# A retention and two mixture-of-experts layers on one core: the front recast in half columns, with its elementwise work off GpSimd

## The chip, the cores and the metric

The kernel runs on one core of a Trainium2 chip. The metric is the device time of one execution in microseconds (us); every time is of the whole kernel unless a stage is named. The engines are named as in the profile: PE (matrix), DVE (vector), ACT (scalar), POOL (GpSimd), SP (which here only issues DMAs). PE's weight loads have a row of their own, PEld.

## What is computed

Three layers follow each other. The first is a retention over two batches of eight heads, 768 steps, head size 64:

```python
for t in range(S):
    state = gamma[None, :, None, None] * state + np.einsum('bhd,bhe->bhde', k[:, :, t], v[:, :, t])
    y[:, :, t] = scale * np.einsum('bhd,bhde->bhe', q[:, :, t], state)
```

Its output, 1536 tokens of 512 numbers, goes to a layer of eight experts (512 to 1024 to 512, relu between). Each token goes to the expert with the largest gate logit (`x @ w_gate`), if that expert's capacity of 384 isn't used up by earlier tokens, and is scaled by the softmax of its logits. The third layer sums four experts of the same size over all tokens, weighted by given probabilities.

## The kernel before

Only the front differs, the part up to the first expert's first matmul. It works through twelve chunks of 128 tokens (six per batch), one iteration of a Python loop each; a f32 matmul appears as two records in PE's rows. The kernel's order is written out by hand: each engine executes its instructions in the order of the code, and waits by semaphore.

For a chunk i the stages are these, by the names of the functions:

- `st_v` multiplies v by a decay per token and head (vg), on POOL.
- `st_S` makes the scores of the eight heads: q and k of two heads lie in the two halves of the 128 partitions, so eight matmuls of 64 rows and 128 columns write two PSUM banks, the two heads of a pair side by side. DVE multiplies by the causal mask (sd).
- `st_U` adds k'v to a running state in PSUM, which ACT copies to `st`; the sixth chunk of a batch has none.
- `st_I` and `st_O` make the output O (transposed): first from the state and q (not in a batch's first chunk), then from sd and vg.
- `st_x` multiplies O by the gate table `gqs` of the chunk, of which there are six, one per chunk of a batch (xT): ACT copies O from PSUM, POOL multiplies; for the last two chunks DVE does both at once.
- `x_pe` multiplies xT by `iw`, identity and gate weights side by side, which gives the tokens in rows and the logits. `x_reduce` adds the four partial logits (two reductions and a step that adds them and takes the maximum), ACT copies the tokens to xk in two pieces, and a DMA writes them to DRAM (xd).
- `x_dve` finds the expert of each token (`ohs`), the running counts (`cum`) and token numbers by expert (`ohk`).
- `r_pe` and `r_dve` give each token its rank within its expert by two small matmuls (R) and compare it with slot numbers (`slot_at`); `g_pe` collects the token number of each slot (slot_ps).

Iteration `it` runs I, U, O and x of chunk it-1, then v of chunk it+1, S of chunk it, the loads of chunk it+3, x_pe of chunk it-2, g_pe of chunk it-4 and r_pe of chunk it-3. SP issues the loads in the code's order: qk (q and k transposed, 512 KB a chunk), kv (k and v in rows, 512 KB), the gate tables (256 KB each), then expert weights; qk and kv have five buffers each. PSUM's eight banks are four that rotate and four with fixed use (slot, u and the two of X). In iteration 8 the first expert weight is split into a high and a low part, ACT then DVE on 128x1024.

After the loop come the last chunks: `late` places tokens of the last two chunks directly, `fetched` those that an indirect DMA gathers from xd, and ACT and DVE split the result for the first expert. Behind that the experts' matmuls begin (`pair`), which the change leaves alone. Lines of the profile: S is L267, U L291, I L310, O L322, X L365, slot_ps L447, R L350 and L351, vg L251, the gate product L337 and L341, xk L384, the step that adds logits L389, the weight split L142 and L143.

## Time and profile before

| | |
|---|---|
| median of three runs | 734.7 us (733.98 to 735.59) |
| the profiled execution | 732.1 us, its span 730.3 us |
| PE busy | 718.0 us, 98% of the span |
| DVE, ACT, POOL busy | 470.6, 337.7, 203.1 us |
| bytes moved by DMA | 92.83 MB |

The span is the time from the first to the last instruction in the trace; what lies around it, 1.8 us in that execution, is start and end. A matmul's row shows when it starts and how long until its result is there; matmuls overlap, so the cost of a stage is read from its start to the start of the next, not from its duration. A number in brackets behind a row is the time for which the engine had nothing to execute before, and what ended that.

### The profile page before, as it was taken

What the parts mean: (1) busy time and instruction counts of PE and PEld (TensorE: products, weight loads), DVE (VectorE), ACT (ScalarE), POOL (GpSimd) and SP (SyncE); (2) the same over time, 40 slices, a digit from 0 to 9 for tenths busy, and PEclk for the clock granted to TensorE, in tenths of its full rate; (3) what the DMA queues carried; (4) which work ended last, traced back from release to release, by engine and by line L of the source; (5) the groups of instructions that cost most, each with busy time, mean ns of one, the idle gap of its engine ahead of it and who ended that gap; (6) DMA issues with size and microseconds to landing.
All of it is one profiled execution on the core that took longest, in us unless ns stands there. A gap on an engine that the chain in (4) does not pass through costs nothing.

```text
span 730.3 us, 11338 instructions
## 1 busy us (share of the span) xinstructions
PE 718.0 (98%) x4425; PEld 656.6 (90%) x4426; DVE 470.6 (64%) x777; ACT 337.7 (46%) x545; POOL 203.1 (28%) x193
## 2 busy tenths in 40 slices
PE   7998999999999999999999999999999999999997
PEld 5887999999999889998889998899998899988896
DVE  3888899898889736455733755763475464557334
ACT  2344677776656433344333445534444333443331
POOL 3653844442054102112332112223322121111103
PEclk9999999999999999999999999999999999999999
DMA  8984887686641310211221112122222312112002
GB/s 329 414 345 135 301 306 237 239 289 226 226 146 34 116 56 32 87 58 58 88 86 58 58 57 88 59 87 87 87 73 76 99 42 87 59 58 84 33 1 86
DMA packets 28026, 92.83 MB, mean 127 GB/s; under 512 B 4097, under 2 KB 4369, under 8 KB 27970
## 3 DMA queue, kind: packets, MB, share of 16 engines
q1 hardware_dynamic: 23042, 81.79, 32.4%
q0 software_dynamic: 3056, 7.05, 2.8%
q10 hardware_dynamic: 1872, 3.24, 1.2%
q8 instruction: 35, 0.57, 0.3%
q14 instruction: 21, 0.17, 0.1%
HBM read 85.72 MB, written 6.34 MB: 126 GB/s over the span
## 4 chain that ended last, share of the span: by engine, by line
PE 88%; DVE 1%; POOL 1%; ACT 0%; issue 0%; POOLq 0%; ACTq 0%
PE o L1213 35%; PE a L1057 17%; PE m L951 15%; PE b L1057 9%; PE m L954 7%; PE bb L1057 5%; POOL out_dram L1225 1%; PE ab L1057 0%; DVE x L856 0%; DVE X L869 0%; ACT X L865 0%; DVE c L1150 0%; POOLq L1410 0%; PE T L769 0%; ACT c L1088 0%
## 5 line engine op out<-in xcount | busy, mean ns | idle before, releaser
L1213 PE MATMUL o<-w,g_c 128*128 128x512 f32 x1152 | 267.4, 390 | 0.0
L1213 PEld LDWEIGHTS o<-w,g_c 128*128 128x128 f32 x1152 | 215.8, 188 | 43.8
L143 DVE TENSOR_TENSOR w<-raw,w 128x1024 fp32r<-128x1024 f32 x128 | 158.2, 1244 | 14.2 <-ACT w L142 14.1
L1057 PE MATMUL a<-X,w 128*128 128x384 f32 x720 | 145.0, 336 | 0.0
L158 POOL TENSOR_TENSOR t<-raw 128x512 f32<-128x512 f32 x28 | 38.8, 1386 | 346.4 <-DMA raw<-b 299.1
L1092 DVE TENSOR_TENSOR c<-b,c 128x384 f32<-128x384 f32 x30 | 16.7, 558 | 181.3 <-PE b L1057 181.3
L142 ACT CAST w<-raw 128x1024 fp32r<-128x1024 f32 x128 | 132.1, 1048 | 2.7 <-DMA raw<-a 1.5
L1057 PEld LDWEIGHTS a<-X,w 128*128 128x128 f32 x720 | 127.4, 188 | 2.6 <-DVE c L1092 0.3
L1088 ACT COPY c<-a 128x384 f32<-128x384 f32 x60 | 28.8, 479 | 196.4 <-PE a L1057 196.4
L1073 ACT ACTIVATE g_c<-c 128x384 fp32r<-128x384 f32 x96 | 50.4, 526 | 65.9 <-DVE c L1092 64.6
L951 PE MATMUL m<-xet,w 128*128 128x432 f32 x256 | 79.1, 371 | 0.8 <-PEq L636 0.8
L951 PE MATMUL m<-h,w 128*128 128x432 f32 x256 | 79.2, 371 | 0.0
L1057 PE MATMUL b<-X,w 128*128 128x384 f32 x360 | 72.0, 334 | 0.0
L954 PE MATMUL m<-h,w 128*128 128x216 f32 x256 | 66.8, 261 | 0.0
L954 PE MATMUL m<-xet,w 128*128 128x216 f32 x256 | 66.7, 261 | 0.0
L625 POOL DMA_INDIRECT xe<-xd,gidx x42 | 52.7, 1255 | 46.2 <-DVE xT L753 34.7
L1057 PEld LDWEIGHTS b<-X,w 128*128 128x128 f32 x360 | 63.5, 188 | 0.0
L1077 DVE SCALAR_TENSOR_TENSOR g_c<-c,g_c 128x384 fp32r<-128x384 f32 x96 | 52.9, 551 | 3.9
L951 PEld LDWEIGHTS m<-xet,w 128*128 128x128 f32 x256 | 48.0, 188 | 2.9 <-PEq L636 1.0
L951 PEld LDWEIGHTS m<-h,w 128*128 128x128 f32 x256 | 48.1, 188 | 1.9
L954 PEld LDWEIGHTS m<-h,w 128*128 128x128 f32 x256 | 48.9, 191 | 0.0
L954 PEld LDWEIGHTS m<-xet,w 128*128 128x128 f32 x256 | 48.9, 191 | 0.0
(158 smaller groups left out, 763.1 us busy)
## 6 DMA issues: line engine op xcount, KB each, us to landing
raw<-a SPq DMA_DIRECT2D x64, 512.0 KB, 4.8
raw<-b SPq DMA_DIRECT2D x64, 512.0 KB, 3.5
qk<-qkv SPq DMA_DIRECT2D x12, 512.0 KB, 8.3
kv<-qkv SPq DMA_DIRECT2D x12, 512.0 KB, 8.3
xd<-xk ACTq DMA_DIRECT2D x12, 256.0 KB, 6.0
gqs<-gqt SPq DMA_DIRECT2D x6, 256.0 KB, 7.5
xe<-xd,gidx POOLq DMA_INDIRECT x44, 4.8
iw<-cst SPq DMA_DIRECT2D x1, 272.0 KB
```

The costliest lines, as they stand in the source:

```text
L142: nc.scalar.copy(w[:, 0], r)
L143: nc.vector.tensor_tensor(out=w[:, 1], in0=r, in1=w[:, 0].bitcast(F32), op=ALU.subtract)
L158: eng.tensor_tensor(out=c[:, 0:2], in0=b[:, 2:4], in1=b[:, 1:3], op=sub)
L625: nc.gpsimd.indirect_dma_start(out=t[:, b], out_offset=None, in_=xq, in_offset=bass.IndirectOffsetOnAxis(ap=gidx[:, b, e:e + 1], axis=0),)
L951: nc.tensor.matmul(out=b2, lhsT=w[0], rhs=x, start=first, stop=last, skip_group_check=True)
L954: nc.tensor.matmul(out=b2[:, 0], lhsT=w[1], rhs=x[:, 0], start=False, stop=last, skip_group_check=True)
L1057: nc.tensor.matmul(out=bk[:, 0:HT], lhsT=w[:, sw, k], rhs=x[:, sx, k], start=(first and m == 0), stop=(m == len(steps) - 1), skip_group_ch ...
L1073: nc.scalar.activation(out=h2[:, 0], in_=src, func=AF.Relu)
L1077: nc.vector.scalar_tensor_tensor(out=h2[:, 1], in0=src, scalar=0.0, in1=h2[:, 0].bitcast(F32), op0=ALU.max, op1=ALU.subtract,)
L1088: nc.scalar.copy(t, bk[:, 0:HT])
L1092: nc.vector.tensor_tensor(out=t, in0=bk[:, 0:HT], in1=t, op=ALU.add)
L1213: nc.tensor.matmul(out=bk, lhsT=h2[:, sh, cols], rhs=w[:, sw, k], start=(q == 0 and m == 0 and (n, t) not in begun), stop=(m == 2), skip_g ...
```

## The change

- **Half columns.** S, X, R and slot_ps are made of matmuls that use 64 columns of the array each. S has sixteen (64 rows by 64 columns, the four quarters of the array in turn) instead of eight, X eight (128 rows by 64 columns) instead of four, R and slot_ps four each instead of two. U, I and O had 64 columns already.
- **Order.** S of chunk `it` stands first in its iteration, ahead of I, U and O of chunk it-1. R is written into X's bank, just ahead of X. kv is loaded two chunks ahead, qk three.
- **Off POOL.** vg of chunks 2 to 11 is eight ACT instructions of 64 columns (POOL for chunks 0 and 1); the gate product is DVE's for every chunk, straight from PSUM; ohk is ACT's.
- **Tables.** One gate table is loaded; POOL makes the other five from it by a factor per partition and head. `iw` is built on chip by two ACT copies out of a smaller table.
- **Smaller steps.** The logits are one reduction over four parts and one maximum, xk one copy; the slot comparison reads 16-bit numbers (`rnk16`). The first weight is split in four parts, one in each of iterations 7 to 10.
- **PSUM.** The front has pairs of banks for S, O and X, one of each, beside slot and u. Before the last chunk's X that pool is closed and another opened, whose tiles wait for the old tiles one by one.

The diff, without the constants' layout on the host:

```diff
-    banks = [f"bank{n}" for n in range(4)]
-    held = ["slot", "u", "x0", "x1"]
+    ph0 = sctx.enter_context(tc.tile_pool(name="ph0", bufs=1, space=PSUM))
+    ps = [fctx.enter_context(tc.tile_pool(name="psa", bufs=1, space=PSUM))]
...
+    def split_part(q):
+        if q == 0:
+            parts.append((raws.pop(0), pw.tile([P, 2, 1024], F32R, tag="w", name="w0")))
+        r, w = parts[0]
+        cols = slice(256 * q, 256 * q + 256)
+        nc.scalar.copy(w[:, 0, cols], r[:, cols])
+        nc.vector.tensor_tensor(
+            out=w[:, 1, cols], in0=r[:, cols], in1=w[:, 0, cols].bitcast(F32), op=ALU.subtract
+        )
...
         load_qk(0)
-        nc.scalar.dma_start(out=cdec, in_=cst[:, 0:C_IW])
+        nc.scalar.dma_start(out=cdec, in_=cst[:, 0:C_U])
         load_kv(0)
         load_qk(1)
-        load_gq(0)
+        load_qk(2)
         load_kv(1)
-        nc.sync.dma_start(out=iw.rearrange("p a b -> p (a b)"), in_=cst[:, C_IW:C_U])
-        load_qk(2)
-        nc.sync.dma_start(out=kc, in_=cst[:, C_U:])
-        load_gq(1)
-        load_kv(2)
+        nc.sync.dma_start(out=gqs[:, 0], in_=gqt)
...
+            if i < 2:
+                nc.gpsimd.tensor_tensor(
...
+            else:
+                for h in range(8):
+                    nc.scalar.activation(
+                        out=vg[:, h], in_=v[:, h], func=AF.Copy, scale=gk[:, i % NCH, h:h + 1]
+                    )
...
-                for j in range(2):
+                for m in range(4):
+                    o, j = 64 * (m >> 1), m & 1
                     r = slice(64 * j, 64 * j + 64)
                     nc.tensor.matmul(
-                        out=bks[j][:, cols], lhsT=qk[r, 1, cols], rhs=qk[r, 0, cols],
-                        start=True, stop=True,
+                        out=bks[j][o:o + 64, cols],
+                        lhsT=qk[r, 1, hp * P + o:hp * P + o + 64], rhs=qk[r, 0, cols],
+                        start=True, stop=True, skip_group_check=True,
                     )
...
-            if i < NT - 2:
-                ot = p2.tile([P, 512], F32, tag="ot", name=f"ot{i}")
-                for j in range(2):
-                    nc.scalar.copy(ot[:, 256 * j:256 * j + 256], bks[j][:, 0:256])
-                nc.gpsimd.tensor_tensor(out=xT, in0=ot, in1=gqs[:, c], op=ALU.mult)
...
+            for j in range(2):
+                cols = slice(256 * j, 256 * j + 256)
+                nc.vector.tensor_tensor(
+                    out=xT[:, cols], in0=bks[j][:, 0:256], in1=gqs[:, c, cols], op=ALU.mult
+                )
...
+            b2 = xbs[i] = two(tag, f"X{i}")
+            if rank is not None:
+                r_pe(rank, b2[:, 1, 448:456])
             for hp in range(KD):
+                for o in (0, 64):
+                    nc.tensor.matmul(
+                        out=b2[o:o + 64, hp // 2, hp % 2 * 256:hp % 2 * 256 + 136],
+                        lhsT=xT[:, hp * P + o:hp * P + o + 64], rhs=iw[:, hp], start=True,
+                        stop=True, skip_group_check=True,
+                    )
...
         for it in range(NT):
+            st_S(it)
             if it >= 1:
                 st_I(it - 1)
                 st_U(it - 1)
                 st_O(it - 1)
                 st_x(it - 1)
             for i in range(it + 1 if it else 0, min(it + 2, NT)):
                 st_v(i)
-            st_S(it)
             if it + 3 < NT:
                 load_qk(it + 3)
-                if it + 2 < NCH:
-                    load_gq(it + 2)
-                load_kv(it + 3)
+            if it == 0:
+                nc.sync.dma_start(out=kc, in_=cst[:, C_U:])
+            if it + 2 < NT:
+                load_kv(it + 2)
...
+                for c in range(1, NCH):
+                    gr = cdec[:, C_GR + 4 * (c - 1):C_GR + 4 * c]
+                    nc.gpsimd.tensor_tensor(
+                        out=gqs[:, c].rearrange("p (m t) -> p m t", m=4),
+                        in0=gqs[:, 0].rearrange("p (m t) -> p m t", m=4),
+                        in1=gr.rearrange("p (m t) -> p m t", t=1).to_broadcast([P, 4, P]),
+                        op=ALU.mult,
+                    )
...
-                x_pe(it - 2)
+                x_pe(it - 2, it - 3 if it >= 3 else None)
...
-            if it == 8:
-                split_w(0)
+            if 7 <= it < 11:
+                split_part(it - 7)
...
+        fctx.close()
+        ps[0] = sctx.enter_context(tc.tile_pool(name="psb", bufs=1, space=PSUM, reuse_waits="tile"))
```

Three places show how the instructions stand now. The first is ACT from the third iteration on (names carry the chunk: st0 and st1 the two states, U0 the state's bank, vg2 chunk 2, xk0 chunk 0). Before:

```order
L296 COPY st0_114<-U0_173 128x256
L336 COPY ot1_244<-O1_0_216 128x256
L336 COPY ot1_244<-O1_1_217 128x256
L384 COPY xk0_270<-X0_0_272 128x2x4x32
L384 COPY xk0_270<-X0_1_273 128x2x4x32
L388 DMA xd_68<-xk0_270 128x512
```

and in the change:

```order
L278 ACTIVATE vg2_226<-kv2_175,cdec_110 128x64 x8
L324 COPY st0_118<-U0_205 128x256
L278 ACTIVATE vg3_288<-kv3_237,cdec_110 128x64 x8
L410 COPY xk0_304<-X0_305 128x4x4x32
L414 DMA xd_68<-xk0_304 128x512
```

The multiplies that wait for a kv now stand ahead of the copies of the state and of xk on the same engine.

The second is PE in the iteration of chunk 4 (numbers as above; O3 from state and q is I, from sd and vg is O). The change has, from X of chunk 1 on:

```order
L395 MATMUL X1_388<-iw_112,xT1_285 64x136 x8
L294 MATMUL S4_417<-qk4_235 64x128 x16
L339 MATMUL O3_436<-qk3_172,st1_119 64x128 x8
L319 MATMUL U0_205<-vg3_288,kv3_237 64x64 x8
L351 MATMUL O3_436<-sd3_325,vg3_288 64x128 x8
L374 LDWEIGHTS onesb_77
L374 MATMUL X2_481<-cum_81,onesb_77 64x8
```

Before, S4 stood behind O3 and ahead of X2, and the R of chunk 1 behind X2 in a bank of its own; now S4 is ahead of I3, and R comes first, into the bank that X2 uses.

The third is SP's queue at the start. Before:

```order
L223 DMA kv1_127<-qkv 128x1024
L236 DMA iw_109<-cst 128x544
L219 DMA qk2_130<-qkv 128x1024
L238 DMA kc_75<-cst 128x452
L226 DMA gqs_108<-gqt 128x512
L223 DMA kv2_134<-qkv 128x1024
```

and in the change:

```order
L244 DMA qk2_130<-qkv 128x1024
L248 DMA kv1_132<-qkv 128x1024
L258 DMA gqs_111<-gqt 128x512
L244 DMA qk3_172<-qkv 128x1024
L496 DMA kc_78<-cst 128x452
L248 DMA kv2_175<-qkv 128x1024
```

qk2 and qk3 moved ahead of kv1 and kv2, iw and the second gate table are gone.

## Rows read from the trace of the kernel before

**Rows 1.** The page: busy time, share of the span and instructions of each engine.

```profile
PE 718.0 (98%) x4425; PEld 656.6 (90%) x4426; DVE 470.6 (64%) x777; ACT 337.7 (46%) x545; POOL 203.1 (28%) x193
```

**Rows 2.** Busy time by stretch: us, then engines, PE clock, DMA share, GB/s.

```profile
30.77:35.52 4.75, 4.32 (x64) 3.80 (x62) 4.36 (x14) 1.29 (x4) 3.19 (x5) 1.00 1.03 418
...
39.95:44.39 4.44, 4.44 (x78) 3.93 (x76) 3.56 (x17) 1.59 (x5) 2.27 (x2) 1.00 1.04 419
...
44.39:49.20 4.81, 4.81 (x80) 4.12 (x78) 3.96 (x12) 2.59 (x7) 2.43 (x2) 1.00 1.03 414
...
68.50:235.00 166.50, 166.40 (x1079) 162.25 (x1080) 152.75 (x208) 114.10 (x165) 71.46 (x58) 1.00 0.66 224
```

**Rows 3.** Timeline of PE, one late iteration: start us, us, what, records.

```profile
39.96 1.16 PE L267 MATMUL S<-qk 64*128 64x128 f32 x16
41.05 1.19 PE L365 MATMUL X<-iw,xT 128*128 128x136 f32 x8
42.08 0.20 PE L447 MATMUL slot_ps<-ohk,at 128*128 128x8 f16 x2
42.13 0.17 PE L350 MATMUL R<-cum,onesb 128*128 128x8 f16 x1
42.16 0.17 PE L351 MATMUL R<-ohs,ub 128*128 128x8 f16 x1
42.25 0.67 PE L310 MATMUL O<-qk,st 64*64 64x128 f32 x16
42.85 0.69 PE L291 MATMUL U<-vg,kv 128*64 128x64 f32 x16
43.37 1.10 PE L322 MATMUL O<-sd,vg 128*64 128x128 f32 x16
44.39 0.38 PE L267 MATMUL S<-qk 64*128 64x128 f32 x2
```

**Rows 4.** Waits from 0 to 53 us: us in total, times, longest.

```profile
PEld S L267 <- issue: 1.5, 9, 0.2
...
PEld U L291 <- issue: 0.7, 4, 0.2
...
PEld S L267 <- DVE ranks L425: 0.6, 1, 0.6
```

**Rows 5.** Timeline of GpSimd: the gated v of chunks 2 and 3.

```profile
15.27 1.11 POOL L251 TENSOR_TENSOR vg<-kv,cdec 128x512 f32<-128x512 f32 x1 [3.26 <-DMA kv<-qkv]
...
19.55 1.04 POOL L251 TENSOR_TENSOR vg<-kv,cdec 128x512 f32<-128x512 f32 x1 [1.94 <-DMA kv<-qkv]
```

**Rows 6.** Timeline of PE, early: the X of chunks 1 and 2.

```profile
19.07 1.19 PE L365 MATMUL X<-iw,xT 128*128 128x136 f32 x8
...
23.45 1.19 PE L365 MATMUL X<-iw,xT 128*128 128x136 f32 x8
```

**Rows 7.** ACT by line, 18 to 53 us: busy us, mean ns | idle before.

```profile
L384 ACT COPY xk<-X 128x256 f32<-128x256 f32 x16 | 5.2, 375 | 11.8 <-DVE lgs L380 11.8
...
L142 ACT CAST w<-raw 128x1024 fp32r<-128x1024 f32 x1 | 1.0, 1046 | 0.9 <-DMA kv<-qkv 0.9
```

**Rows 8.** DVE by line, 18 to 53 us.

```profile
L272 DVE TENSOR_TENSOR sd<-S,cdec 128x512 f32<-128x512 f32 x16 | 10.3, 686 | 4.3 <-PE S L267 4.3
...
L389 DVE CUSTOM_DVE_ANT_0 lgs<-lgs,part 128x8 f32<-128x8 f32 x8 | 5.0, 619 | 0.3
```

**Rows 9.** Timeline of the end of the front.

```profile
53.75 0.76 DVE L341 TENSOR_TENSOR xT<-O,gqs 128x256 f32<-128x256 f32 x2
...
55.75 0.20 PE L447 MATMUL slot_ps<-ohk,at 128*128 128x8 f16 x2
...
57.80 1.15 PE L322 MATMUL O<-sd,vg 128*64 128x128 f32 x16
...
68.52 0.44 PE L951 MATMUL m<-xet,w 128*128 128x432 f32 x1 [0.83 <-PEq L636]
```

**Rows 10.** The page: DMA issues, KB each, median us to landing.

```profile
gqs<-gqt SPq DMA_DIRECT2D x6, 256.0 KB, 7.5
```

More of the change, by code (lines that the diff above doesn't have):

```diff
@@ L303, in st_I @@
             c = i % NCH
-            live[i]["o"] = [bank(f"O{i}_{j}") for j in range(2)]
+            o2 = two("o2", f"O{i}")
+            live[i]["o"] = [o2[:, j] for j in range(2)]
             q = live[i].pop("q")
@@ L446, in g_pe @@
             for b in range(SL // P):
-                nc.tensor.matmul(
-                    out=slot_ps[:, b], lhsT=at[:, b * P:(b + 1) * P], rhs=ohk[:, i],
-                    start=(i == 0 and b == 0), stop=True, skip_group_check=True,
-                )
+                for o in (0, 64):
+                    nc.tensor.matmul(
+                        out=slot_ps[o:o + 64, b], lhsT=at[:, b * P + o:b * P + o + 64],
+                        rhs=ohk[:, i], start=(i == 0 and b == 0), stop=True,
+                        skip_group_check=True,
+                    )
         def braid(*seqs):
@@ L494, in tile_retention_moe_moe, with late, fetched @@
             if it >= 3:
-                r_pe(it - 3)
                 seqs.append(r_dve(it - 3))
             braid(*seqs)
-            if it == 8:
-                split_w(0)
+            if 7 <= it < 11:
+                split_part(it - 7)
+        k01, k23 = range(2), range(2, KD)
+        def late(i, ks):
+            for k in ks:
+                nc.tensor.matmul(
+                    out=xt0[k // 2][:, k % 2], lhsT=xks[i][:, k * P:(k + 1) * P], rhs=at0[i],
+                    start=(i == NE and k % 2 == 0), stop=True, skip_group_check=True,
+                )
+        def fetched(ks):
+            for b in range(SL // P):
+                w = min(SM - b * P, P)
+                for k in ks:
+                    nc.tensor.matmul(
+                        out=xt0[k // 2][:, k % 2, b * P:b * P + w],
+                        lhsT=xe0[:, b, k * P:(k + 1) * P], rhs=ident[:, 0:w],
+                        start=False, stop=True, skip_group_check=True,
+                    )
         st_I(NT - 1)
-        x_pe(NT - 2)
-        r_pe(NT - 3)
+        x_pe(NT - 2, NE - 1, True, "s2")
         st_O(NT - 1)
-        braid(r_dve(NT - 3))
-        g_pe(NT - 4)
-        g_pe(NT - 3)
+        g_pe(NE - 2)
+        braid(r_dve(NE - 1))
+        g_pe(NE - 1)
         st_x(NT - 1)
@@ L550, in tile_retention_moe_moe @@
         slot_at(NT - 1)
-        late(NE + 1)
+        late(NT - 1, range(KD))
         g_pe(NT - 2)
         g_pe(NT - 1)
-        for b in range(SL // P):
-            fetched(b, range(2))
+        fetched(k01)
         nc.vector.tensor_scalar(
@@ L573, in tile_retention_moe_moe @@
         nc.vector.tensor_copy(rows, slot_ps.rearrange("p b e -> p (b e)"))
-        rps = bank("rows", "u")[:, 0:NB4 * E1]
+        rps = held("u", "rows")[:, 0:NB4 * E1]
         for b in range(NB4):
@@ L580, in tile_retention_moe_moe @@
             )
-        for b in range(SL // P):
-            fetched(b, range(2, KD))
+        fetched(k23)
     def offsets():
```

192 lines of the change are left out of this document (94 added, 98 removed).

## The prediction

> **What bounds the kernel now.** I read the page first: PE is busy 718.0 of 730.3 us [rows 1], so time can only come out of stretches in which PE waits or pays for something other than streaming columns. The busy time by stretch [rows 2] finds the place. From 68.50 to 235.00 us PE is busy 166.40 of 166.50 us, and the change leaves that code as it is; the clock is 1.00 throughout. What is left is the front, 68.5 us until the first expert's matmul [rows 9]. There two resources are full at once: PE works 4.44 of 4.44 us in an ordinary iteration, and the DMA share stands at 1.03 to 1.04 with 414 to 419 GB/s in the three iterations shown.
>
> A full PE is not a PE that streams columns. The timeline of one iteration [rows 3] gives S 1.09 us (39.96 to 41.05), X 1.03, four small matmuls 0.17, I 0.60, U 0.52, O 1.02. O's sixteen records of 128 columns, two array halves side by side, and I's sixteen, four quarters side by side, contain a change of shape behind them: the list of waits has an "issue" gap of about 0.17 us before S in 9 iterations and before U in 4 [rows 4]. Without it I takes 0.43 and O 0.85. That is how I price half and quarter pieces.
>
> **The steady iteration.** S becomes 32 records in quarters: twice I's 0.43, 0.86 us. X becomes sixteen half-column records of 136 columns: O's 0.85 x 136/128 = 0.90. The small ones go from four to eight; the starts from 42.08 (two) over 42.13 to 42.16 are about 0.025 apart [rows 3], so 0.17 becomes about 0.27. I 0.43, U 0.52 and O 0.85 stay. Two changes of array rows remain, before U and before S, 0.17 each. Sum 0.86 + 0.43 + 0.17 + 0.52 + 0.85 + 0.27 + 0.90 + 0.17 = 4.17; as no gap stood where the small ones meet I [rows 3], I take 0.03 off: **4.14 us against 4.44, 0.30 less**. Bounds: 3.97 if the entry into S is as free as that into I is now; 4.34 if S and X keep 0.1 us of start-up each. From the X of chunk 2 to that of chunk 9 are seven periods: **-2.1 us, bounds -3.3 to -0.7.**
>
> DVE gains the gate product, 0.76 us for two [rows 9], and loses one half-reduction and the combining step; ACT gains eight small multiplies and the token product and loses two copies. DVE then has sd 2 x 0.69 [rows 8], xT 0.76 and some 1.5 us of small steps, 3.6; ACT 0.37 + 1.4 + 0.60 + 0.2, 2.6 (prices below). Both are under 4.14 and cost nothing, while PE's 4.14 covers them. The weight split in four adds a quarter of 1046 ns on ACT [rows 7] and 0.3 us on DVE in four iterations, still covered.
>
> **The stalls that go.** Two iterations are longer than their work. 30.77:35.52 lacks I (0.60 of 4.44) and still takes 4.75: 0.9 us over, of which the S that waits for the ranks is 0.6 [rows 2, 4]. 44.39:49.20 contains the whole first weight split and takes 4.81: 0.37 over. In the first, DVE's small steps are stretched: the combining step L389 takes 619 ns on average over 8 elements a partition [rows 8], while GpSimd works beside it. GpSimd is empty after its tables, some 12 to 18 us, and the split is in quarters: **-1.25 us, bounds -1.25 to 0.**
>
> **The start, which the change makes later.** GpSimd began vg of chunks 2 and 3 at 15.27 and 19.55, as their kv landed [rows 5]. On the DMA queue kv2 now has qk3 ahead of it, but no second gate table and no 272 KB of iw: 4.35 MB up to its end against 4.28, at 0.415 MB/us 0.2 us later. For kv3 it is 5.40 against 5.59 MB: 0.45 us earlier, 19.1. But vg is now on ACT, and ACT is in order: behind vg3 stands the copy xk0, and X1 needs its bank, of which there is one pair. An ACT copy of 256 columns has a mean of 375 ns and 5.2/16 = 325 ns of busy time; with 1046 ns for 1024 columns a column is 0.87 ns [rows 7]. So 64 columns take 0.21 alone and about 0.16 in a row: eight between 1.3 and 1.7, I take 1.4. xk in one piece of 512 is 0.60. X1 can start at 19.1 + 1.4 + 0.6 + 0.1 = 21.2, R0's 0.1 in front of it makes 21.3, against 19.07 [rows 6]: 2.2 late. The next iteration, not held by kv4, wins 0.3 back: X2 **1.9 us late** against 23.45. S3 is done before X1 in both orders, so the comparison is fair. The lower bound is +0.6 (kv3 lands at 18.0, as it would if transfers behind it overtook it less; 1.3 for vg); the upper is +3.5 (every multiply as dear as the nearest row, 375 ns, eight of them 3.0).
>
> **The tail.** From the small ones at 55.75 to O's end at about 58.85, I, X, O and the switches lie [rows 9]. The same prices give 0.35 less there, the rank comparison from 16 bit and one reduction less perhaps 0.1, the doubled small matmuls cost 0.05 back: **-0.4, bounds -0.9 to +0.3.** Then X11, ranks, gathered rows and the first expert form the old chain. The pool change asks for waits by tile, on tiles that the same steps had to finish anyway: nothing, covered by xT11 and xk10. The smaller tables on chip cost ACT 0.7 us at 6 us, when it is idle.
>
> **Sum:** -2.1 - 1.25 + 1.9 - 0.4 = -1.85. The profiled execution took 732.1 us and would take 730.25; the median of the three runs is 734.7, 2.6 higher, so I forecast **732.8 us** (own range 731 to 734.3).
>
> **Rivals.**
> *The transfers set the pace.* The full DMA engines [rows 2] speak for it, and five gate tables of 256 KB [rows 10] and 0.19 MB net of iw are 1.50 MB or 3.6 us. Against it: the front's PE is also full. If each chunk waits for its kv, -3.6 - 0.4 gives 730.7. 0.18.
> *The small halves eat the gain.* If a 16-bit half load with its tiny matmul paces like an O record, 0.85/16 = 0.053 instead of 0.025, eight of them cost 0.2 more per iteration: period 4.34, -0.7 - 1.25 + 1.9 - 0.4 = -0.45, so 734.25, no change. Against it stand the 0.025 us now, for full-width loads. No row shows a 16-bit half load. [...] 0.19.
> *ACT becomes the bound, slower.* If each 64-column multiply costs 375 ns, ACT has 0.37 + 3.0 + 0.6 + 0.2 = 4.2 us an iteration and 4.5 in the four with a weight quarter. It decides from about 0.35 us each. Then +3.5 at the start, three periods at -0.24, four at +0.06, -1.25 and -0.4: +1.4, so 736.1. 0.13.
> *The change doesn't do what it says:* halves don't run side by side. S and X would double, +1.8 us over eight iterations, 749. I, U and O, which do run so [rows 3], speak against it. 0.03.
>
> **How the numbers follow.** Forecast 0.47 (0.40 of it faster by over 0.2%, 1.5 us, about what a measurement can tell from no change; 0.07 within), transfers 0.18 faster, small halves 0.19 (0.03 faster, 0.13 same, 0.03 slower), ACT 0.13 (0.01 same, 0.12 slower), not side by side 0.03 slower: faster 0.61, same 0.21, slower 0.18. The range reaches from below the transfer case, all good bounds together being -4.85, to just over ACT's: 729.3 to 736.4.
>
> **What would show it.** Right: a period near 4.14 between late S, no "issue" gap before S, X1 starting near 21.2 and ended by xk0, no S waiting for ranks, the first expert near 66.6. Wrong: a period of 4.3 with gaps at the small matmuls; vg multiplies near 375 ns with PE idle on ACT; X waiting for kv through vg in late iterations; PE gaps after the first expert's start.

## The result, and the profile after

The changed kernel takes 741.85 us (median of four runs, 741.4 to 745.3) against 734.34 us for the kernel before beside it: a ratio of 1.0112, interval 1.0077 to 1.0146. It is slower by 1.1%, with the whole interval above 1; the forecast was 732.8 us and its range ended at 736.4. The profiled execution after took 741.4 us, 9.3 more than the one before.

The page's first part shows that PE works as long as before [rows 1]; the 9.3 us are idle time of PE.

```profile
PE 717.5 (97%) x4762; PEld 655.8 (89%) x4763; DVE 468.1 (63%) x765; ACT 353.3 (48%) x610; POOL 184.1 (25%) x178
```

Reading off the start of each X and of the first expert's matmul gives where they arise:

| | before | after | difference |
|---|---|---|---|
| X1 | 19.07 | 21.10 | +2.03 |
| X2 | 23.45 | 25.15 | +1.70 |
| X2 to X9 | 31.27 | 30.97 | -0.30 |
| X9 to first m | 13.80 | 17.07 | +3.27 |
| first m | 68.52 | 73.19 | +4.67 |
| from there to the end of the span | 661.81 | 666.42 | +4.61 |

**The steady iteration is what was forecast.** Busy time by stretch of the kernel after (columns as in [rows 2]): the first and the fourth row hold one undisturbed iteration each, 4.06 and 4.07 us with PE full, against 4.44 [rows 2].

```profile
26.57:30.63 4.06, 4.06 (x104) 3.87 (x104) 3.56 (x15) 3.35 (x14) 0.00 (x0) 1.00 0.95 332
37.86:44.34 6.48, 4.46 (x108) 3.98 (x105) 3.48 (x15) 3.74 (x15) 0.00 (x0) 1.00 1.03 408
44.34:49.13 4.79, 4.29 (x105) 3.96 (x105) 4.03 (x16) 3.81 (x14) 0.00 (x0) 1.00 0.89 349
49.13:53.20 4.07, 4.07 (x109) 3.88 (x105) 3.31 (x14) 3.05 (x11) 0.00 (x0) 1.00 0.23 89
71.61:73.38 1.77, 0.24 (x2) 0.22 (x2) 1.26 (x6) 1.68 (x3) 0.88 (x1) 1.00 0.10 32
73.19:235.00 161.81, 159.01 (x1034) 154.12 (x1035) 144.07 (x193) 107.14 (x154) 68.60 (x57) 1.00 0.69 229
```

Between them stand two long ones: 6.48 us with PE busy 4.46, and 4.79 with 4.29. In the last row PE is busy 159.01 of 161.81 us behind the first m, where before it was full [rows 2]: 2.8 of the 4.6 us lost behind the front are idle there.

**The start.** PE's and ACT's timelines of the kernel after, at X1, answer to [rows 5, 6]:

```profile
18.31 0.67 PE L339 MATMUL O<-qk,st 64*64 64x128 f32 x16 [1.33 <-ACT st L324]
...
21.04 0.20 PE L374 MATMUL X<-cum,onesb 128*64 128x8 f16 x2 [0.52 <-ACT xk L410]
...
21.10 0.31 PE L395 MATMUL X<-iw,xT 128*64 128x136 f32 x1
```

```profile
15.98 2.02 ACT L278 ACTIVATE vg<-kv,cdec 128x64 f32<-128x64 f32 x8 [5.41 <-DMA kv<-qkv]
17.90 0.35 ACT L324 COPY st<-U 128x256 f32<-128x256 f32 x1
18.50 2.02 ACT L278 ACTIVATE vg<-kv,cdec 128x64 f32<-128x64 f32 x8 [0.25 <-DMA kv<-qkv]
20.42 0.56 ACT L410 COPY xk<-X 128x512 f32<-128x512 f32 x1
```

vg2 waits 5.41 us for its kv, with the copy of the state behind it that PE waits 1.33 us for; then vg3 and xk0 stand before X1, whose bank is xk0's.

**Two holes that no engine accounts for.** PE's timeline around them:

```profile
38.79 0.49 PE L339 MATMUL O<-qk,st 64*64 64x128 f32 x9
40.72 0.45 PE L339 MATMUL O<-qk,st 64*64 64x128 f32 x7 [1.44 <-issue]
...
44.34 1.10 PE L294 MATMUL S<-qk 64*64 64x128 f32 x32 [0.59 <-PE X L395]
...
47.00 0.45 PE L351 MATMUL O<-sd,vg 128*64 128x128 f32 x4 [0.50 <-issue]
```

The first falls between two matmuls of the same step, whose operands are those of the nine before. The list of waits calls it "issue": the engine waited for nothing that the profile shows. Between the last load or matmul ahead of it and the first behind it lie 1.70 us. Of the DMA queues, one moved a single packet at that time, and it is not data (page's third part, for the stretch 38.5 to 39.5; columns: packets, MB, share of the 16 engines):

```profile
q1 hardware_dynamic: 93, 0.33, 80.7%
...
q8 instruction: 1, 0.02, 6.0%
```

PE's instructions come in packets of 16,384 bytes on queue 8: 38 of them (0.62 MB, page's third part) in the whole span, for 4762 matmuls and 4763 loads. This one ended at 39.48, the next at 45.69; PE went on 1.23 and 1.31 us later.

**ACT stands in line.** Its timeline in that iteration:

```profile
38.69 0.57 ACT L410 COPY xk<-X 128x512 f32<-128x512 f32 x1
41.60 0.34 ACTq L414 DMA_DIRECT2D xd<-xk  x1
41.99 0.30 ACT L436 ACTIVATE ohk<-ohs,kc 128x8 f16<-128x8 f16 x1 [2.74 <-DMA xd<-xk]
42.20 0.39 ACT L162 CAST w<-raw 128x256 fp32r<-128x256 f32 x1
42.49 0.36 ACT L324 COPY st<-U 128x256 f32<-128x256 f32 x1
42.76 2.02 ACT L278 ACTIVATE vg<-kv,cdec 128x64 f32<-128x64 f32 x8
```

The write of xk is issued at 41.60, 2.3 us after xk was ready: an earlier write with the same semaphore, issued at 32.55, lands only at 41.53, and the new one waits for it (not for the write between the two, issued at 35.63, which has another). Everything behind it on ACT waits too: ohk, a weight quarter, the state, and vg, whose eight multiplies take 2.02 us. By the list of waits from 0 to 57 us (columns as in [rows 4]) DVE's half of the split waits for ACT's:

```profile
ACT ohk L436 <- DMA xd<-xk: 4.0, 2, 2.7
...
DVE w L163 <- ACT w L162: 3.9, 4, 2.5
...
PEld O L339 <- issue: 2.6, 2, 1.7
```

DVE stands before w until ACT has written its quarter, at 42.6, and begins sd at 42.96, two pieces of 0.68 us. The S of chunk 9 needs the bank that sd reads: it starts at 44.34, 0.59 us late. The row names X, PE's own step, but X had been done, and sd ends at 44.2 to 44.3.

**The end of the front.** PE's and DVE's timelines there (fetched rows, then the first m):

```profile
69.86 0.68 PE L554 MATMUL T0x<-ident,xe 128*128 128x88 f32 x4 [0.59 <-DMA xe<-xd,gidx]
70.38 0.32 PE L623 MATMUL rows<-rows,rep 128*128 128x8 f16 x7
70.56 1.10 PE L554 MATMUL T0x<-ident,xe 128*128 128x128 f32 x8
73.19 0.43 PE L997 MATMUL m<-xet,w 128*128 128x432 f32 x1 [1.53 <-ACT w L150]
```

```profile
72.25 0.61 DVE L834 TENSOR_TENSOR xet<-T0x,xet 128x432 fp32r<-128x432 f32 x1 [0.51 <-ACT xet L830]
72.77 0.27 DVE L841 TENSOR_SCALAR gidx<-rows,small 128x56 int32<-128x56 f32 x1
```

xet, the operand of the first m, is done at 72.86. PE, which has to wait here for a semaphore ahead of the first load, passes at 73.08, just after gidx has read the tile `rows`, and the load starts at 73.16: that tile lies in the bank of u, and the first expert's output takes that bank. The hole is 1.77 us long; in the kernel before it was 1.08.

**Behind the front.** ACT's timeline of the first expert:

```profile
83.89 0.52 ACT L1024 COPY tsum<-m 128x432 f32<-128x432 f32 x1 [3.64 <-PE m L1000]
```

DVE ended its last step at 81.79, and both wait for a matmul whose last record starts at 80.51; the copy starts 3.4 us after that. No row says what was late. PE then stops twice for lack of h and xet, and the second expert starts 2.9 us later behind the first than it did before.

### The profile page after: what moved, and what is told of

The parts are those of the page before. It is cut to its first block, busy times and chain, and to the rows that moved or that the text cites. A ratio compares the mean times of both kernels' runs of the same rounds, so it can differ in the third digit from the quotient of the medians.

```text
span 739.6 us, 12019 instructions
## 1 busy us (share of the span) xinstructions
PE 717.5 (97%) x4762; PEld 655.8 (89%) x4763; DVE 468.1 (63%) x765; ACT 353.3 (48%) x610; POOL 184.1 (25%) x178
## 4 chain that ended last, share of the span: by engine, by line
PE 84%; DMA 6%; DVE 4%; ACT 2%; issue 1%; POOL 1%; SPq 0%; POOLq 0%; ACTq 0%; DVEq 0%
PE o L1259 35%; PE a L1103 17%; PE m L997 13%; PE b L1103 8%; PE m L1000 6%; PE bb L1103 5%; DMA xd<-xk 2%; DMA kv<-qkv 2%; DMA raw<-a 1%; DVE sd L300 1%; DMA xe<-xd,gidx 1%; DVE w L151 1%; POOL out_dram L1271 1%; ACT xk L410 0%; PE ab L1103 0%
## 5 line engine op out<-in xcount | busy, mean ns | idle before, releaser
L151 DVE TENSOR_TENSOR w<-raw,w 128x1024 fp32r<-128x1024 f32 x127 | 156.2, 1239 | 14.7 <-ACT w L150 14.4
L671 POOL DMA_INDIRECT xe<-xd,gidx x42 | 51.6, 1228 | 51.5 <-DVE xT L799 38.5
```

What stands on the lines that cost most here:

```text
L151: nc.vector.tensor_tensor(out=w[:, 1], in0=r, in1=w[:, 0].bitcast(F32), op=ALU.subtract)
L671: nc.gpsimd.indirect_dma_start(out=t[:, b], out_offset=None, in_=xq, in_offset=bass.IndirectOffsetOnAxis(ap=gidx[:, b, e:e + 1], axis=0),)
```

## Experiments

Ratios are to the kernel before, measured beside each run, where it took 732.0 to 734.4 us, so the times in us are not compared from row to row; X1, X9, the first m (us from the span's start) and the stretch behind it are of the profiled execution. The changed kernel itself was run again (e12): 1.0076 against 1.0112. A difference of 0.3% between two ratios is therefore read with care, and the milestones of the front, which agree within 0.3 us between the change and e12, are read first.

| run | us | ratio, interval | X1 | X9 | first m | behind |
|---|---|---|---|---|---|---|
| before | | 1 | 19.07 | 54.72 | 68.52 | 661.81 |
| after | 741.85 | 1.0112, 1.0077-1.0146 | 21.10 | 56.12 | 73.19 | 666.42 |
| e12 | 738.49 | 1.0076, 1.0060-1.0091 | 21.07 | 56.11 | 73.41 | 664.36 |
| e3 | 734.12 | 1.0027, 1.0017-1.0036 | 19.55 | 56.29 | 70.17 | 662.54 |
| e4 | 740.75 | 1.0119, 1.0102-1.0136 | 21.65 | 56.01 | 72.60 | 665.62 |
| e15 | 744.02 | one run, before 732.03 | 21.49 | 57.56 | 76.47 | 665.79 |
| e6 | 738.64 | 1.0094, 1.0077-1.0110 | 21.37 | 56.00 | 73.43 | 662.67 |
| e10 | 743.71 | 1.0129, 1.0114-1.0144 | 20.90 | 56.62 | 75.01 | 666.56 |
| e2 | 736.48 | 1.0055, 1.0038-1.0072 | 20.04 | 55.52 | 71.85 | 664.62 |
| e5 | 738.91 | 1.0082, 1.0055-1.0109 | 21.21 | 56.63 | 72.79 | 664.73 |
| e1 | 742.50 | 1.0145, 1.0124-1.0165 | 21.19 | 57.51 | 76.42 | 663.79 |
| e7 | 734.69 | 1.0039, 1.0027-1.0052 | 18.59 | 55.33 | 70.44 | 661.85 |
| e8 | 738.91 | 1.0063, 1.0049-1.0078 | 19.41 | 54.50 | 71.53 | 664.92 |
| e9 | 742.04 | 1.0093, 1.0079-1.0107 | 21.61 | 55.98 | 72.39 | 668.17 |
| e11 | 732.95 | 1.0004, 0.9995-1.0013 | 19.65 | 53.81 | 68.23 | 662.19 |
| e13 | 736.87 | 1.0026, 1.0009-1.0044 | 20.17 | 54.68 | 70.02 | 665.43 |
| e14 | 734.91 | 1.0009, 0.9993-1.0025 | 19.55 | 55.09 | 68.89 | 665.85 |

### Half columns and order apart: e3 and e4

**e3**: the kernel before, with half columns in S, X, R and slot_ps alone.

```diff
-                for j in range(2):
+                for m in range(4):
+                    o, j = 64 * (m >> 1), m & 1
...
-                        out=bks[j][:, cols], lhsT=qk[r, 1, cols], rhs=qk[r, 0, cols],
+                        out=bks[j][o:o + 64, cols],
+                        lhsT=qk[r, 1, hp * P + o:hp * P + o + 64], rhs=qk[r, 0, cols],
```

> The kernel before, with S, X, rank and slot matmuls in half columns and nothing else of the change. If half columns alone are worth 0.3 to 0.38 us in each of eleven iterations, as the changed kernel's steady period of 4.06 against 4.44 says: 734.3 less 3 to 4, 730.3 to 731.3. Theory I: PE's instruction blocks are used up sooner and PE shows holes of 0.5 to 1.7 us without a semaphore while the front's transfers fill the DMA engines: 732.5 to 734.5. Theory W has no say: 661.8 after the front stays.

**e4**: the change, with whole columns in these four steps (the same edit backwards).

> The changed kernel, with S, X, rank and slot matmuls in whole columns as before. Theory I: PE's holes at 39.0 (1.7 us) and 46.3 (0.5 us) are gone, the period is 4.4 again, which gives back about as much as the holes cost: 740.5 to 742.5. Rival (the holes come from ACT's queue or the transfers and have nothing to do with PE's rows): the holes stay, the period is 4.4: 743.5 to 745. Theory W: 666 after the front in both cases.

The busy time by stretch, of one undisturbed iteration of e3 and of two of e4:

```profile
50.90:55.25 4.35, 4.35 (x106) 3.82 (x104) 3.35 (x16) 1.67 (x5) 2.28 (x2) 1.00 0.27 101
```

```profile
39.41:43.84 4.43, 4.43 (x79) 3.93 (x76) 3.59 (x14) 3.47 (x14) 0.00 (x0) 1.00 1.02 409
43.84:48.28 4.44, 4.44 (x80) 3.93 (x77) 3.67 (x15) 3.48 (x14) 0.00 (x0) 1.00 1.02 410
```

So before 4.44, halves alone 4.35, order alone 4.43, both 4.06. The gain belongs to the two together. From the starts of the steps, a change of the shape in which the array is used (S to X, O to S and I to U in the kernel before, I to U in the change) puts about 0.20 us between the start of a step's last record and that of the next step, 0.14 to 0.17 more than lies between two records of one step; a step in the same shape comes 0.05 to 0.06 behind (S to I, U to O and O to X in the change), and one behind the small matmuls in another shape 0.10 (slot_ps to S in the change). Halves without the order, or the order without halves, leave three such changes in an iteration, as many as before; both together leave one.

e3 lost the gain elsewhere: its X9 is 1.57 us later than before. It too has a hole of 1.59 us at 38 us, but PE's and DVE's timelines of e3 show another cause:

```profile
37.99 0.43 PE L312 MATMUL O<-qk,st 64*64 64x128 f32 x2
39.74 0.66 PE L312 MATMUL O<-qk,st 64*64 64x128 f32 x14 [1.32 <-DVE sd L274]
```

```profile
36.90 1.19 DVE L422 TENSOR_TENSOR cum<-cum,ohs 128x8 f16<-128x8 f16 x1
38.01 1.08 DVE L425 TENSOR_SCALAR ohk<-ohs,kc 128x8 f16<-128x8 f16 x1
39.01 1.28 DVE L274 TENSOR_TENSOR sd<-S,cdec 128x512 f32<-128x512 f32 x2
```

The third record writes another bank, free when the first of two sd has read it, at about 39.7, and PE starts at once. DVE was late because two steps over 8 elements took 1.19 and 1.08 us (0.16 and 0.22 in the timeline of the kernel before at 36.0), with GpSimd at work beside it. That hole falls in the very stretch of PE's instructions in which the change has its first, so e3 doesn't show whether half columns alone would have met it. e4, with whole columns and all else of the change, has no hole between 22 and 57 us; so the change's two holes come with its half columns.

### What the hole is: e15, with e6 and e10

**e15**: the change, with PE's instructions shifted against the program: five warm-up matmuls of 512 columns instead of nine, and fifty of 8 columns (each is one load and one matmul, so 92 records more).

```diff
-WARM0 = 9
+WARM0 = 5
...
+        for _ in range(50):
+            nc.tensor.matmul(
+                out=bk[:, 0:8], lhsT=fill[:, 0:P], rhs=fill[:, 0:8], start=True, stop=True
+            )
```

> The change with one edit: of the nine warm-up matmuls of 512 columns at the start five stay, and fifty of 8 columns are added, so that every later instruction of PE stands about 100 records further along PE's stream; the work of the front is the same. Theory A (PE waits for the next 16-KB block of its own instructions): the two holes keep their place in the stream and leave their place in the program, by 100 records towards the start. The first, of 1.5 to 2.2 us, then falls inside the X of chunk 5 (L395), near 37.3 us, instead of inside the O from state and q (L339, 39.01 to 40.71); the second, of 0.7 to 1.1 us, inside the S of chunk 8 (L294), instead of at the O from sd and vg (47.00). Rival B (the holes belong to that step: a late operand or the transfers at that time): both stay at L339 and L351. No difference of time is asked of this run.

PE's timeline of e15:

```profile
33.08 0.43 PE L343 MATMUL O<-qk,st 64*64 64x128 f32 x3 [0.53 <-issue]
...
38.11 1.12 PE L399 MATMUL X<-iw,xT 128*64 128x136 f32 x15
40.73 0.23 PE L475 MATMUL slot_ps<-ohk,at 128*64 128x8 f16 x4 [1.50 <-issue]
...
44.95 0.86 PE L298 MATMUL S<-qk 64*64 64x128 f32 x18
46.95 0.55 PE L298 MATMUL S<-qk 64*64 64x128 f32 x11 [1.12 <-issue]
```

Both holes left their steps: the first now opens at the end of X5 (38.95 to 40.73, 1.78 us), the second inside S8 (45.55 to 46.95, 1.39 us), and a third has appeared at 32.28 (0.80 us). Counted in matmuls and loads from the start they stand before numbers 1201, 1455 and 1708; in the kernel after, before 1453 and, the second, 254 later. With PE's semaphore instructions counted too, the holes of e15 open behind instructions 1217, 1473 and 1729, those of the change behind 1473 and 1729. So the place in the stream stays, the place in the program goes, and exactly 256 instructions lie between two holes, for one packet of 16,384 bytes. The operands of the steps in which they open had long been there. Each hole ends 1.3 to 1.5 us after a packet on queue 8. **PE had run out of instructions.**

The 256 instructions of a packet are called a block here. At most borders between two blocks no hole opens: none does with whole columns in e4 between 22 and 57 us, and of the nine borders that the change passes between 10 and 59 us only two have one, near 39 and 46 us, which cost 1.7 and 0.7 us. With 155 records per 4.43 us a block lasts some 7.3 us. With half columns it is 208 records per 4.06 us, 4.95 us a block, and from a block's first record to the first of the next one pass up to 7.7 us in e15 (33.07 to 40.73): in the six blocks that it enters between 8 and 41 us the packet begins 2.8 to 5.3 us behind the entry (1.5 to 4.3 in the change between 10 and 41 us), takes 0.95, and at a hole PE goes on 1.3 to 1.5 us later.

Two runs were to show whether the full DMA engines delay that packet. **e6** asks for the expert weights raw1 to raw4 later, **e10** for all of them at iteration 11, with the split behind the loop.

```diff
-                load_w(min(4, it - 5))
+                load_w(max(1, it - 8))
```

```diff
-            if it >= 6:
-                load_w(min(4, it - 5))
+            if it == NT - 1:
+                load_w(4)
...
-            if 7 <= it < 11:
-                split_part(it - 7)
...
+        split_w(0)
```

> The changed kernel with raw1 to raw4 of the weights asked for from iteration 10 on and not from iteration 7; raw0 as it is. Theory I with its second half (PE's instruction blocks come over the same DMA engines and are late only where the transfers fill these): PE's holes at 39.0 (1.7 us) and 46.3 (0.7 us) shrink to under 0.5 together, X of chunk 9 starts 1.5 to 3 us earlier than 56.1, and what the late weights cost comes after the front. Rival (PE runs dry because its rows are used up faster than one fetch can follow, with or without transfers): both holes stay as long as they are. The time itself may go either way: 739 to 745.

> The changed kernel with all five weight loads of the front put into iteration 11 and the first split at the front's end. Only the front before 56 us counts here, the time itself will be 2 to 6 us longer. Theory I with its second half (a block comes late only where transfers fill the DMA engines): with 2.5 MB less between 28 and 56 the last kv lands earlier, the hole near 46 is gone, the one near 39 is under 1 us, and the wait from the start of a block to the fetch of the next falls from 4.0 to 4.3 us to under 2 there. Rival (a fetch takes that long whatever else is moved): both holes stay at 1.5 to 2.2 and 0.7 to 1.2 us.

Neither took the transfers away: in e6 the DMA share stayed between 0.95 and 1.04, and in e10 SP, which no wait held back, issued the weights at 36.2 to 42.5 us all the same. The holes stayed in e6 (1.62 and 1.08); e10 has one of 2.21 us, and no second. But behind that one its granted clock was 0.50 from 41.3 to 44.7 us, the block lasted from 41.03 to 47.49, and its packet, begun at 44.87, came in time. The share before e10's late packet was 0.71 at 34 to 36 us and 0.92 at 36 to 38, and the packet was no earlier; that speaks against full engines as the cause, and doesn't settle it. Why a packet starts 2.8 to 5.3 us after its block is entered, and 0.7 to 2.2 us in the three that e15 enters between 46 and 57 us, stays open. The packet hardly follows the entry: in fourteen runs the block entered between 33.1 and 36.0 us got its packet at 37.7 to 39.3.

### The start: e2, e7, e13

**e2**: vg of all chunks on GpSimd (`if i < 2` becomes `if True`).

> The changed kernel, with the gate multiply of every chunk (vg) on GpSimd as one instruction, not as eight on ACT from chunk 2 on. Theory A: the second X, at 21.1 in the changed kernel, starts by 20.0, S of iteration 9 no longer waits 0.6, and the first expert matmul comes 2 to 3 us earlier than 73.2; time 738 to 739.5. Theory W: the front may move by 1 us, the stretch after it stays at 666; 740.5 to 741.5. Theory I: PE's hole of 1.7 us near 39 stays, since no instruction of PE changes.

X1 starts 1.06 us earlier, at 20.04, and the ratio falls from 1.0112 and 1.0076 to 1.0055. The holes stay (1.50 and 1.13).

**e7** puts together what the runs so far had shown: vg on GpSimd, one gate table an iteration instead of five at once, three constant conversions on ACT, kv1 and gqs ahead of qk2, the tail's rank behind X10, and `rows` in the bank of R.

```diff
         load_qk(1)
-        load_qk(2)
         load_kv(1)
         nc.sync.dma_start(out=gqs[:, 0], in_=gqt)
+        load_qk(2)
...
-            if i < 2:
+            if True:
...
-                for c in range(1, NCH):
...
+            if it + 1 < NCH:
+                c = it + 1
...
-        rps = held("u", "rows")[:, 0:NB4 * E1]
+        rps = rb[:, 64:64 + NB4 * E1]
```

> The changed kernel with vg of every chunk on GpSimd, one gate table per iteration, the three conversions of iteration 2 on ACT, kv1 asked for before qk2, the tail's rank matmuls behind X of chunk 10, and the rows in bank rb. If the causes found so far add up: from e2 (ratio to before 1.0055, some 4 us above) X of chunk 1 starts 1 us earlier, the tail is 0.7 us shorter, the hole before the first expert matmul 0.7 us shorter, and the 1.4 to 1.6 us at the lower clock go: ratio 0.998 to 1.001. PE's two holes near 38 and 45 stay under Theory I and are then all that is left of the loss. If the front is bound by its transfers, X of chunk 9 does not come earlier than in e2 (55.5): ratio 1.002 to 1.004.

X1 is at 18.59, 2.5 us earlier than in the change and 0.5 earlier than before, and nothing is lost behind the front (661.85). With two ratios of 1.0076 and 1.0112 for the change, 1.0039 recovers half to two thirds. What is left stands in holes of the same kind: 1.12, 1.51 and 1.13 us, before records 692, 1449 and 1701, all three 1.2 to 1.5 us after a packet.

**e13**: e11 (below) with gqs, qk2, kv1 in this order.

> The mixed version with quarters, its first transfers in another order: the gate table, then qk2, then kv1, where it had kv1, the table, qk2. PE works without a break from S of chunk 2 on (12.0 there), so if S of chunk 2 starts earlier by 0.6 to 1.1 us the whole front does: first expert matmul at 67.1 to 67.6, ratio to before 0.998 to 0.9995. If U of chunk 1 then waits for kv1 and its multiply, nothing or a loss of up to 0.5 us: ratio 1.000 to 1.001. [...]

The S of chunk 2 came later, 12.52 against 12.00, and X1 with it, 20.17 against 19.65. But in the execution profiled PE's granted clock was 0.67 and 0.50 just there. Its busy time by stretch, the clock in the last column but two:

```profile
8.00:10.00 2.00, 1.67 (x16) 1.52 (x16) 0.00 (x0) 0.00 (x0) 0.02 (x1) 0.67 0.96 309
10.00:12.00 2.00, 2.00 (x28) 1.95 (x28) 1.29 (x2) 0.37 (x1) 0.23 (x1) 0.50 1.00 367
```

In e11 the clock is 1.00 in both. The S of chunk 1 started earlier than in e11, 8.34 against 8.71; its U then lasted 0.90 us instead of 0.52, its O 1.57. So what the order of the three loads is worth isn't shown.

### The bank of rows: e5

```diff
-        rps = held("u", "rows")[:, 0:NB4 * E1]
+        rps = rb[:, 64:64 + NB4 * E1]
```

> The changed kernel with one thing moved: the small 'rows' matmuls write into free columns of the rank bank rb and no longer into bank u, which after the pool change lies under the first expert's first output, so that its first matmul waits for the copy of gidx from there. [...]

Expected were a hole of about 1.1 us before the first m, 662 to 663 us behind the front and a ratio of 1.006 to 1.009, and 665 to 666 us and 1.010 to 1.012 if late weights made the loss there. The hole is 0.98 us instead of 1.77, and the m no longer waits for gidx: PE's timeline of e5 has the first m at 72.79, 0.41 ahead of the gidx that DVE's has at 73.20. The ratio is 1.0082; behind the front it took 664.73 us, though the granted clock was 1.00 there (72.79 to 81.79 us).

```profile
72.79 0.47 PE L997 MATMUL m<-xet,w 128*128 128x432 f32 x1 [0.70 <-PEq L682]
```

```profile
73.20 0.27 DVE L841 TENSOR_SCALAR gidx<-R,small 128x56 int32<-128x56 f32 x1
```

### The split and DVE's own code: e1, e8, e11

**e1**: the change, with the first weight split whole at iteration 8.

```diff
-            if 7 <= it < 11:
-                split_part(it - 7)
+            if it == 8:
+                split_w(0)
```

> The changed kernel, with the first weight split whole in iteration 8 as before, not in quarters over iterations 7 to 10. Theory W (late weights: the last quarter falls in iteration 10, so raw4 is asked for at 56.1 and no longer at 46.4): raw4 is issued near 46 to 48 and the stretch after the first expert matmul, 666.4 long in the changed kernel and 661.8 before, comes back to about 662; time 737 to 738. Theory A (ACT, which multiplies v and the gates, is the bound of the front): the stretch after the front keeps its 666 and the time stays at 741 to 742. Theory I (PE runs out of instructions, since half columns nearly double its rows): the same, and PE's hole of 1.7 us at 39.0 that no semaphore explains is still there.

Worse: the hole before the first m grew to 3.49 us. The stretch behind it, 663.79, is within what the change itself shows in e12 (664.36), so that late weights cost time there isn't shown. The same again in **e8**, which is e7 with whole columns up to iteration 8 and halves from 9, and the split in two halves in iterations 8 and 9:

```diff
+                for j in range(2) if i <= 8 else ():
...
-                for m in range(4):
+                for m in range(4) if i > 8 else ():
...
-            if 7 <= it < 11:
-                split_part(it - 7)
+            if 8 <= it < 10:
+                split_part(it - 8)
```

> The combined version of the run before, with three more parts: whole columns up to iteration 8 and half columns only from iteration 9 on, in the tail O of chunk 11 in the banks of S and X of chunk 10 in those of O, and the first weight split in two halves in iterations 8 and 9. Theory I (blocks of some 254 PE records are used up in 4.9 us in half columns and in 7.3 in whole ones, and a block takes 6 to 6.5 us to come while the transfers fill the DMA engines): no PE hole over 0.5 us without a semaphore between 36 and 48, the front 1.5 to 2.5 us shorter than the 70.4 of the combined version; ratio to before 0.998 to 1.001. Rival (the front is bound by its transfers or by DVE beside GpSimd, and the holes only took up slack): the holes go and the front stays at 69.5 to 70.5; ratio 1.002 to 1.004.

PE no longer stands still at a block's border, but S waits 1.15 and 0.83 us for sd behind the larger pieces, and the first m comes after a hole of 3.44 us. DVE's and then ACT's timeline of e8:

```profile
70.87 1.12 DVE L846 TENSOR_TENSOR xet<-T0x,xet 128x432 fp32r<-128x432 f32 x2 [4.24 <-ACT w L150]
```

```profile
67.29 0.52 ACT L842 CAST xet<-T0x 128x432 fp32r<-128x432 f32 x1 [3.07 <-PE T0x L564]
68.41 0.52 ACT L842 CAST xet<-T0x 128x432 fp32r<-128x432 f32 x1 [0.60 <-PE T0x L564]
```

ACT's first half of xet is done at 67.81, and DVE, with nothing left to do, starts its half at 70.87; packets of 8 KB of instructions, of queue 14, end at 68.77, 69.34 and 69.78 (which engine's they are the trace doesn't show). Just there DVE passes a branch (in the change at 69.31 to 69.68). That suggested the same cause on another engine, a guess: the number of DVE's instructions ahead decides whether its code is there. **e11** is e8 with the split in quarters again, over iterations 7 to 10: two more instructions on DVE, smaller pieces.

```diff
-            if 8 <= it < 10:
-                split_part(it - 8)
+            if 7 <= it < 11:
+                split_part(it - 7)
```

> The mixed version with the multiply on GpSimd, its first weight split in quarters over iterations 7 to 10 as in the changed kernel, not in two halves. [...]

Expected were a hole of 0.9 to 1.1 us and a ratio of 0.997 to 1.001 by that guess, and 3.4 us and 1.004 to 1.006 if the hole came from the banks of O and X in the tail. The waits of S went, and the hole before the first m went from 3.44 to 1.07 us. DVE's timeline of e11:

```profile
67.38 1.24 DVE L846 TENSOR_TENSOR xet<-T0x,xet 128x432 fp32r<-128x432 f32 x2 [1.70 <-ACT xet L842]
```

e1 and e10, with a split of one piece, had 3.49 and 3.55; the change, e5 and e6, in quarters, at most 1.77. All the traces agree: where DVE has executed 194 or 195 instructions before its first step on xet (e1, e8, e9, e10), that step comes 3.2 to 3.5 us behind the branch; with 196 to 206, in the other thirteen, at most 0.6 us behind ACT's half. The edit that adds two instructions undoes the wait, but it also makes the pieces smaller; DVE was not shifted by itself as e15 shifts PE, so this cause fits and isn't shown. Over eleven runs e11 takes as long as the kernel before: 1.0004, 0.9995 to 1.0013.

**e9** is e8 with vg of chunks 3 and on on ACT; **e14** is e11 with whole columns everywhere.

```diff
-            if True:
+            if i < 3:
```

```diff
-                for m in range(4) if i > 8 else ():
+                for m in range(4) if i > 99 else ():
```

> The same as the run beside it, but with the gate multiply on ACT from chunk 3 on, as in the changed kernel from chunk 2 on, so that GpSimd rests after the gate tables. If GpSimd's multiplies slow DVE's small steps (cd takes 227 ns in the changed kernel and 396 in the combined one, between 30 and 60) and that is what binds: faster than the run beside it by 0.5 to 1.5 us. If ACT's order binds (its eight multiplies stand behind the write of xd, which waits for an earlier write): slower by 1 to 2 us, with waits of S for DVE.

> The mixed version with quarters (ratio 1.0004), with whole columns in every iteration and in the tail. If half columns pay where the transfers have ended (periods of 4.05 to 4.1 against 4.43 from iteration 9 on, where a block comes within 3 us): slower by 1.0 to 1.5 us, ratio 1.0018 to 1.0025. If they pay nowhere (the tail and the last iterations wait for DVE and for ACT anyway): ratio 1.000 to 1.001. Either way no PE hole over 0.5 us without a semaphore.

e9 has X1 at 21.61 against e8's 19.41: vg on ACT costs the start 2.2 us here, though vg2 is on GpSimd. e14's X11 is 1.09 us later than e11's (59.97, 58.88) and its first m 0.66: so much are the halves worth from iteration 9 on, a hole of 0.91 us that e11 still has at a block's border (47.44 to 48.35) included. In time the two can't be told apart (1.0009 and 1.0004).

### The change again: e12

> The changed kernel again, as it is. Its first profile showed ACT and DVE waiting 3.1 us for the third output of the first expert at the full clock, which no row explains, and 666.4 us after the first expert matmul. If that belongs to the code: again a wait of ACT for PE of over 3 us at 10.7 us behind the first expert matmul. If it was that one execution: the stretch after the first expert matmul is 662 to 665 here, and what it loses shows as a lower clock behind the hole of 1.77 us or as waits for weights. Time 739 to 742 either way, ratio 1.009 to 1.013.

The front repeats: X9 at 56.11, the holes 2.02, 1.08 and, before the first m, 1.77. What lies behind does not: ACT's wait of 3.6 us is absent, but the granted clock drops. Busy time by stretch of e12, the clock in the last column but two:

```profile
73.00:75.00 2.00, 1.59 (x7) 1.56 (x8) 1.86 (x10) 1.33 (x2) 1.63 (x2) 0.71 0.35 68
75.00:77.00 2.00, 2.00 (x9) 1.88 (x9) 1.77 (x2) 0.00 (x0) 1.45 (x2) 0.50 0.61 219
77.00:79.00 2.00, 2.00 (x14) 1.95 (x13) 0.29 (x1) 1.27 (x3) 1.67 (x2) 0.94 0.86 252
```

At 0.50 PE executes 9 matmuls in 2 us, at 0.94 it executes 14, and 15 at 1.00 (79 to 81 us). The three means together are worth 3.4 us at 0.50. A pair of m's matmuls comes every 0.57 us in e8 at 0.50 and every 0.31 in e11 at 1.00; at about half the pace the 3.4 us cost some 1.7 (an estimate). Two executions of one kernel lose 4.6 and 2.6 us behind the front, each in its own way.

## Why the prediction was wrong, step by step

- **The steady iteration** ("4.14 us against 4.44"): right, 4.06 and 4.07, and the changes of shape were the reason, which e3 and e4 show by 4.35 and 4.43. The rival of the small halves fell: their starts are 0.02 to 0.03 apart (29.43, 29.46, 29.49), so its 0.053, the pace of O's records, doesn't hold for them.
- **"-2.1 us, bounds -3.3 to -0.7"** for seven periods and **"-1.25"** for the stalls: this is where it failed. Seven iterations at that pace, two of them short of a step, would have taken 27.6 us (5 x 4.07 + 3.60 + 3.63). They took 30.97: 1.75 us too much from X5 to X6 and 1.37 from X6 to X7, the two holes, the second with the S that waits, and 0.27 at the beginning. By the work alone 3.7 us would have been gained, with 3.35 forecast; the holes and the late S took most of it back, and 0.30 was left. The sum put the supply of instructions at nothing, without a reason: it never asked whether a third more of them in an iteration, 208 for 155, could be brought in a shorter period. The trace of before had the count of records and the packets of queue 8.
- **DVE and ACT "cost nothing, while PE's 4.14 covers them"**: wrong in two ways. The multiplies were put at 1.4 us for eight and take 2.02, so ACT is busy 3.35 of 4.06 us, with 2.6 forecast; and busy time says nothing of an engine in order whose next instruction waits. One write of xd that waited for an older one held ohk, a weight quarter and vg for 2.3 us, and with the split DVE and S.
- **The start** ("2.2 late", X2 "1.9 us late"): right in size (2.03 and 1.70), by luck. X1 was ended by xk0, as said (0.52 us), but the multiplies of vg3 began at 18.50, not at 19.1, and took 2.02 us, not 1.4: two errors that cancel. That vg2 waits 5.41 us for its kv, with the copy of the state behind it, was not in the sum.
- **The tail** ("-0.4, bounds -0.9 to +0.3"): +3.27. O and X of one bank pair each make I11 wait 0.79 us for lgs, R waits 0.50 for ohs inside X10, slot_ps 0.52 for at; X9 to X10 is 3.32 us, with the rank behind X10 2.58 (e7).
- **The pool change, "nothing, covered by xT11 and xk10"**: wrong. The tile that mattered was another one, `rows`, which now lies under the first expert's output: 0.8 us (e5: 0.98 for 1.77).
- **"The change leaves that code as it is"**, so no term behind the front: wrong by 4.6 us in this execution, 2.6 in e12. The clock explains some 1.7 of e12's (the estimate above); for the 3.4 us of ACT and DVE in this one no row names a cause, and e13 and e14 lost 3.6 and 4.0 us in the same stretch in the executions profiled (stops of 1.15 and 1.95, 1.17 and 1.95 us). The cause stays open.

The forecast of faster rested on a sum that held for each step in isolation. The losing side, ACT as the bound, was listed, but with its price on vg alone, and its 736.1 too is below the result.

## What to carry to other kernels

Splitting matmuls to fill the array made more instructions per microsecond here, 208 records in 4.06 us for 155 in 4.43: count the instructions in a packet (256 in 16,384 bytes), the time they last (4.95 us), and compare it with the interval at which PE's packets arrive (6.2 us from the one that ended at 39.48 to the next), since a hole inside a step with the releaser "issue" was the sign that they had run out (1.70 us near 39). When work is moved to an engine that executes in order, price what its next instruction may wait for (the write of xk that waited 2.3 us for an older one), not only its busy time. A gap at the end of a stage costs more than its length where the clock falls behind it: in e12 3.4 us at 0.50 followed a hole of 1.77.

## What the runs showed that was not expected

- **The clock after a gap.** Behind the hole before the first m the granted clock fell to 0.50 for 3 to 7 us, in e1, e2, e4, e8, e9, e10, e12 and e15, whose holes had 1.77 us or about 3.5, in e9 1.11 behind a wait of 2.42. It fell as well behind e10's hole of 2.21 us at 39 us, and not behind one of 2.23 us in e5 at the same place. In the execution of the change whose profile stands above and in e6 it stayed at 1.00 behind the same 1.77 us, and behind holes of at most 1.1 us in the kernel before, e3, e5, e7, e11, e13 and e14 too.
- **Changing the array's shape** puts about 0.20 us between the starts of two steps (0.199 from I to U in the change and in the kernel before), and 0.05 to 0.06 lie there where it stays. What happens in between no row shows.
- **DVE's cd was shorter beside an idle GpSimd, and that didn't decide.** It takes 227 ns in the change between 30 and 57 us, 425 in e7, where GpSimd works beside it, and 519 in the kernel before (30 to 54 us). e7 is nevertheless the faster of the two.
